# The first layer of the 128-row remainder tiles: four weight chunks in one accumulator bank, with one set of element-wise operations

## The chip, the cores and the metric

The kernel runs on one core of a Trainium2 chip. The metric is the device time of one execution in microseconds (us). The core has five engines, each with its own queue of instructions that it works off in order: TensorE (PE, matrix products, results in the PSUM accumulator memory; PEld is its loading of weights), VectorE (DVE), ScalarE (ACT), GpSimd (POOL) and SyncE (SP), which here issues the DMA transfers. PSUM is cut into banks of 512 fp32 columns on 128 partitions.

## What is computed

Two parts, one behind the other. First, causal attention with a decay on 8 batches of 8 heads, 576 rows and 64 columns per head. Second, on the 4608 x 512 result, a two-layer block with a hard-swish between the layers:

```python
scores = scale * np.matmul(q, k.transpose(0, 1, 3, 2))
decay = cum[:, :, :, None] - cum[:, :, None, :]          # cum: running sum of log f
attn = softmax(where(causal, -1e9, scores + decay))
x = matmul(attn, v)          # rearranged to 4608 rows x 512

h = x @ w_in                 # 512 -> 2048
relu6 = np.clip(h + 3.0, 0.0, 6.0)
g = h * relu6 / 6.0
out = g @ w_out              # 2048 -> 512
```

The kernel keeps fp32 accuracy with fp16 products: each operand is split into a high and a low fp16 part, and a product is three matmuls (high by high, high by low, low by high).

## The kernel before

The program goes through the heads one after another (`VH`). For each it emits the scores, the softmax, the transposition by DMA and the product with v. While it does this for batch b+1, the two-layer block of batch b is emitted in small units between the steps of the heads: `fill` keeps a credit, and lets the unit at the head of the list `units` advance by one `yield`, which costs the number yielded (`H_COST` is 1.05). The framework then settles the order of each engine's instructions with a simulated timeline, priorities and the free buffers, and sets the semaphores. The order on an engine is therefore near the program's, but two units, or a unit and a head, may be interleaved.

A batch has 576 rows, 512 + 64. `moe_tile` does the 512 rows: 16 units `h_unit` for the 16 chunks (`fc`) of 128 of the 2048 hidden columns, and then 4 units `out_unit` of 128 rows. The 64 rows left of two neighbouring batches are put together in the tile `xT[2]`, and `moe_rest(k)` does these 128 rows, with a column of scales for each batch. It is called four times: three times between the heads, after `moe_tile` of batch 1, 3 and 5, and once at the very end, where no attention is left. The profile names its tiles `ph_r`, `r_r` and `po_r`, those of `moe_tile` `ph`, `r` and `po`.

One `h_unit` consists of:

- 12 matmuls (lines 777 to 779; 4 chunks of 128 input columns, three products each) into one PSUM tile `ph` from `mm_tile`;
- for each segment of rows with a scale of its own, a Relu on ACT (line 784) from `ph` into the SBUF tile `r`. A full unit has one segment of 512, a unit of `moe_rest` two of 64;
- on DVE, the minimum with 6 and the product with `ph` (line 787). It is the last reader of the bank;
- on ACT, the copy to fp16, the high part of `gT` (line 789);
- on DVE, the low part of `gT`, as a difference (line 790). It is the last reader of `r`.

`out_unit` then multiplies `gT` by the second layer's weights, 48 matmuls of 512 columns (lines 800 to 802), in the order of the 16 chunks.

`mm_tile` hands out three banks: two in the pool `ps_m`, and at each third call the one of `ps_t`. The tile `r` has three buffers. A unit of `moe_rest` takes a whole bank and a whole buffer too, and uses 128 of its 512 columns. It yields 0.525, a full one 2 x 1.05.

Lines of the heads that the profile shows beside this: 611 and 614 (`pn`, scores on PE), 622 (mask and row maximum on DVE), 634 and 648 (exponential and fp16 copy on ACT), 651, 657 and 662 (low part, on DVE or POOL), 694 to 699 (`pav`, product with v, which waits for the transposing DMA `pT<-ring`), 399 and 400 (splitting v on ACT and DVE).

Of the kernel before, what the change touches and what calls it, by code (L numbers as in the profile page):

```python
# [11 lines left out]
F32 = mybir.dt.float32  # L12
F32R = mybir.dt.float32r
I32 = mybir.dt.int32
AF = mybir.ActivationFunctionType
ALU = mybir.AluOpType
# [4 lines left out]
def kernel(  # L21
# [10 lines left out]
    nc = tc.nc  # L32
# [7 lines left out]
    P = 128  # L40
# [4 lines left out]
    NCC = DM // P  # L45
    NFC = DFF // P
    TT = 512
# [3 lines left out]
    CG = 2.0 ** -22  # L51

    cpool = ctx.enter_context(tc.tile_pool(name="cpool", bufs=1))
    p2 = ctx.enter_context(tc.tile_pool(name="p2", bufs=2))
# [16 lines left out]
    bias_r = cpool.tile([P, 1], F32, name="bias_r")  # L71
# [11 lines left out]
    H_COST = 1.05  # L83
# [48 lines left out]
    w1 = [cpool.tile([P, NCC, DFF], F16, name=f"w1{i}") for i in range(2)]  # L132
    w2 = cpool.tile([P, NFC + 1, 2, DM], F16, name="w2")
    gT = cpool.tile([P, 2, NFC, TT], F16, name="gT")


    xT = [cpool.tile([P, NCC, TT // P, 2, P], F16, name=f"xT{i}") for i in range(3)]
# [13 lines left out]
    NG = 4  # L151
    SC = cpool.tile([P, 80], F32, name="SC")
    SV, IV, UO, UX, A1 = 0, 8, 16, 24, 32
# [47 lines left out]
    def scol(c):  # L201
        return SC[:, c:c + 1]
# [174 lines left out]
    def moe_scale_in(b, j):  # L377
        nc.vector.scalar_tensor_tensor(
            scol(A1 + NG * b + j), scol(IV + b), CG, scol(I1 + j), op0=ALU.mult, op1=ALU.mult
        )  # L380

    def moe_scale_out(b):
        nc.vector.scalar_tensor_tensor(
            scol(UO + b), scol(IV + b), 1.0 / (6.0 * CG), scol(I1R), op0=ALU.mult, op1=ALU.mult
        )
        nc.vector.tensor_tensor(scol(UO + b), scol(UO + b), scol(I2), op=ALU.mult)
        if b % 2 == 1:
            nc.vector.tensor_copy(SC[:64, UX + b:UX + b + 1], SC[:64, UO + b - 1:UO + b])
            nc.vector.tensor_copy(SC[64:, UX + b:UX + b + 1], SC[64:, UO + b:UO + b + 1])
# [196 lines left out]
    o = 0  # L586
# [176 lines left out]
    def mm_tile(name, three):  # L763

        turn[0] += 1
        if three and turn[0] % 3 == 0:
            return ps_t.tile([P, TT], F32, tag="tr", name=name)
        return ps_m.tile([P, TT], F32, tag="mm", name=name)

    def h_unit(x, fc, c0, c1, segs, three, name):  # L770

        nw = c1 - c0
        ph = mm_tile(f"ph_{name}_{fc}_{c0}", three)[:, :nw]
        fs_ = slice(fc * P, (fc + 1) * P)
        for cc in range(NCC):
            xh, xl = (x[:, cc, c0 // P:c1 // P, hl] for hl in range(2))
            nc.tensor.matmul(ph, w1[0][:, cc, fs_], xh, start=(cc == 0), stop=False)  # L777
            nc.tensor.matmul(ph, w1[0][:, cc, fs_], xl, start=False, stop=False)  # L778
            nc.tensor.matmul(ph, w1[1][:, cc, fs_], xh, start=False, stop=(cc == NCC - 1))  # L779
            if cc == 1 and nw == TT:  # L780
                yield H_COST
        r = p2.tile([P, TT], F32, tag="rt", name=f"r_{name}_{fc}_{c0}", bufs=3)[:, :nw]
        for a, e, b in segs:
            nc.scalar.activation(  # L784
                r[:, a:e], ph[:, a:e], AF.Relu, bias=bias_r, scale=scol(A1 + NG * b + fc * NG // NFC)
            )
        nc.vector.scalar_tensor_tensor(r, r, 6.0 * CG, ph, op0=ALU.min, op1=ALU.mult)  # L787
        g0 = c0 if x is not xT[2] else 0
        nc.scalar.copy(gT[:, 0, fc, g0:g0 + nw], r)  # L789
        nc.vector.tensor_tensor(  # L790
            gT[:, 1, fc, g0:g0 + nw], r, gT[:, 0, fc, g0:g0 + nw], op=ALU.subtract
        )
        yield H_COST if nw >= TT // 2 else H_COST / 2

    def out_unit(s, col, rows, three, name):

        po = mm_tile(f"po_{name}_{s}", three)
        ts_ = slice(s * P, (s + 1) * P)
        for fc in range(NFC):
            nc.tensor.matmul(po, gT[:, 0, fc, ts_], w2[:, fc, 0, :], start=(fc == 0), stop=False)  # L800
            nc.tensor.matmul(po, gT[:, 0, fc, ts_], w2[:, fc, 1, :], start=False, stop=False)  # L801
            nc.tensor.matmul(po, gT[:, 1, fc, ts_], w2[:, fc, 0, :], start=False, stop=(fc == NFC - 1))  # L802
            if fc % 2 and fc < NFC - 1:
                yield 2.0 - H_COST
        o = p2.tile([P, DM], F32, tag="o", name=f"o_{name}_{s}")
        nc.scalar.activation(o, po, AF.Copy, scale=scol(col))
        p = 0
        for r0, r1 in rows:
            nc.sync.dma_start(out[r0:r1, :], o[p:p + r1 - r0])
            p += r1 - r0  # L810
        yield 2.0 - H_COST

    def moe_tile(b, c0=0, c1=TT):

        for fc in range(NFC):
            j, new = divmod(fc, NFC // NG)
            if new == 0 and c0 == 0:
                while j not in w_in_done:
                    next(w_in_q, None)
                moe_scale_in(b, j)  # L820
            yield from h_unit(xT[b % 2], fc, c0, c1, [(0, c1 - c0, b)], b > 0 or c0 > 0, f"{b}")
        if b == 0:
            for _ in wq:
                pass
        if c0 == 0:
            moe_scale_out(b)
        for s in range(c0 // P, c1 // P):
            r = S * b + (64 if b else 0) + s * P
            yield from out_unit(s, UO + b, [(r, r + P)], b > 0 or s * P >= QA, f"{b}")

    def moe_rest(k):

        b = 2 * k
        for fc in range(NFC):
            yield from h_unit(
                xT[2], fc, k * P, (k + 1) * P, [(0, 64, b), (64, P, b + 1)], True, f"r{k}"
            )
        r = S - 64 if b == 0 else S * b
        yield from out_unit(0, UX + b + 1, [(r, r + 64), (S * (b + 1), S * (b + 1) + 64)], True, f"r{k}")

# [62 lines left out]
    def one(*a):  # L903
        yield from moe_tile(*a)

    def done(v):
        kind, n = VH[v]
        if kind == "A":
            if n == NPAIR - 1:
                units.append(one(0, 0, QA))  # L910
            return
        b, h = divmod(n, H)
        if h == H - 1:
            units.append(one(b, QA if b == 0 else 0, TT))
            if b % 2:
                units.append(moe_rest(b // 2))
# [4 lines left out]
    for i, (kind, n) in enumerate(VH):  # L921
        b, h = divmod(n, H)
        if kind == "A":
            b = h = 0
# [23 lines left out]
        ph = next(sg)  # L948
# [78 lines left out]
```

## Time and profile before

| | us |
|---|---|
| three runs | 1109.0 median, 1106.02 to 1109.42 |
| the profiled execution | 1104.82 |
| its span, first to last instruction | 1102.8 |
| PE busy in it | 1021.7 |
| DVE, ACT, POOL busy | 737.4, 619.0, 405.6 |

The mean granted PE clock of the profiled execution is 0.976. A busy time is the union of the times in which an engine had an instruction under way. Matmuls are pipelined: a row gives a matmul of 512 columns some 380 ns, though in an unbroken sequence the next one starts earlier, so rates are better read from starts. In the page's first part a row is an engine; in its second, the span is cut into 40 equal slices with a digit for the busy tenths of each.

### The profile page before, as it was taken

To read this page: it belongs to the slowest core of one execution; us is meant where nothing else is said; L and a number is where in the kernel's file an instruction comes from. 1 tells how busy PE (TensorE), PEld (TensorE's weight loads), DVE (VectorE), ACT (ScalarE), POOL (GpSimd) and SP (SyncE) were. 2 spreads that over 40 slices of the span, in tenths; PEclk is the share of its full clock that TensorE was granted. 3 is DMA by queue.
4 is the path that set the end of the run, shared out by engine and by line. 5 is a ranking of instruction groups with operands and counts; after the bars stand their busy time and mean duration, and the time that the engine had idled before them with its cause. 6 is when DMAs were issued, how large, how long until landed. Compare 5 with 4: busy or idle time off the path is not lost.

```text
span 1102.8 us, 21497 instructions
## 1 busy us (share of the span) xinstructions
PE 1021.7 (93%) x7650; PEld 612.0 (55%) x7650; DVE 737.4 (67%) x1983; ACT 619.0 (56%) x1333; POOL 405.6 (37%) x505
## 2 busy tenths in 40 slices
PE   2899977899999699999999799999999799999997
PEld 2677844755555655555555655555555655444445
DVE  7879899786967856867875767846895756305202
ACT  4778567655744765555744666545754756205205
POOL 7343566344444522444443632444443510000000
PEclk9889989999999999999999899999999999999999
DMA  8965557864866582567566781656657643100000
GB/s 255 295 183 181 141 125 147 187 135 95 180 129 134 124 182 50 116 138 166 114 132 131 151 167 39 122 124 171 119 118 139 110 81 57 26 29 10 1 29 20
DMA packets 259158, 133.80 MB, mean 121 GB/s; under 512 B 226948, under 2 KB 228540, under 8 KB 259052
## 3 DMA queue, kind: packets, MB, share of 16 engines
q1 hardware_dynamic: 259052, 132.44, 53.8%
q8 instruction: 60, 0.98, 0.4%
q14 instruction: 46, 0.38, 0.1%
HBM read 47.93 MB, written 9.73 MB: 52 GB/s over the span
## 4 chain that ended last, share of the span: by engine, by line
PE 73%; DVE 11%; DMA 5%; ACT 4%; issue 3%; POOL 2%; SPq 0%; ACTq 0%; DVEq 0%; POOLq 0%
PE ph L777 9%; PE ph L779 9%; PE ph L778 9%; PE po L800 9%; PE po L802 9%; PE po L801 9%; PE pn L611 3%; PE pn L614 3%; DMA pT<-ring 2%; DVE ring L651 2%; DVE pp L622 2%; PE po_r L800 1%; PE pav L705 1%; PE po_r L801 1%; PE po_r L802 1%
## 5 line engine op out<-in xcount | busy, mean ns | idle before, releaser
L634 ACT ACTIVATE pp<-pp,nb 128x192 f32<-128x192 f32 x280 | 138.7, 553 | 140.2 <-DVE nb L628 120.4
L777 PE MATMUL ph<-xT,w 128*128 128x512 f16 (+1 forms) x576 | 199.9, 358 | 1.5 <-DVE r L787 1.3
L801 PE MATMUL po<-w,gT 128*128 128x512 f16 x512 | 192.4, 382 | 8.9 <-DVE w L295 8.9
L779 PE MATMUL ph<-xT,w 128*128 128x512 f16 (+1 forms) x576 | 199.4, 357 | 0.0
L778 PE MATMUL ph<-xT,w 128*128 128x512 f16 (+1 forms) x576 | 199.1, 357 | 0.0
L800 PE MATMUL po<-w,gT 128*128 128x512 f16 x512 | 190.4, 383 | 3.7 <-DVE e_v L187 2.1
L802 PE MATMUL po<-w,gT 128*128 128x512 f16 x512 | 192.4, 382 | 0.0
L651 DVE TENSOR_TENSOR ring<-pp,ring 128x128 f16<-128x128 f32 (+2 forms) x216 | 130.2, 614 | 70.9 <-ACT ring L648 69.8
L787 DVE SCALAR_TENSOR_TENSOR r<-r,ph 128x512 f32<-128x512 f32 (+1 forms) x144 | 89.4, 621 | 96.2 <-ACT r L784 95.5
L622 DVE CUSTOM_DVE_ANT_0 pp<-pn,W 128x192 f32<-128x192 f32 x280 | 123.4, 482 | 30.8 <-PE pn L614 26.6
L461 POOL TENSOR_TENSOR T<-ST,T 64x576 fp32r<-64x576 f32 (+1 forms) x68 | 102.8, 1512 | 102.2 <-DMA T<-TK 87.5
L784 ACT ACTIVATE r<-ph,bias_r,SC 128x512 f32<-128x512 f32 (+1 forms) x144 | 104.0, 727 | 47.6 <-PE ph L779 45.8
L611 PE MATMUL pn<-TK,TQ 68*128 68x192 f32 x336 | 121.3, 376 | 8.1 <-issue 6.9
L790 DVE TENSOR_TENSOR gT<-r,gT 128x512 f16<-128x512 f32 (+1 forms) x144 | 105.9, 740 | 29.3 <-ACT gT L789 28.0
L778 PEld LDWEIGHTS <-w 128*128 128x128 f16 x832 | 82.6, 100 | 70.6 <-issue 25.4
L789 ACT CAST gT<-r 128x512 f16<-128x512 f32 (+1 forms) x144 | 81.4, 567 | 61.9 <-DVE r L787 61.5
L449 POOL TENSOR_SCALAR TK<-ST 64x576 fp32r<-64x576 f32 (+1 forms) x68 | 49.0, 721 | 181.6 <-PE pn L611 143.5
L648 ACT CAST ring<-pp 128x192 f16<-128x192 f32 x280 | 114.5, 452 | 1.5 <-DMA pT<-ring 1.5
L779 PEld LDWEIGHTS <-w 128*128 128x128 f16 x832 | 82.6, 100 | 56.9 <-issue 4.8
L614 PE MATMUL pn<-T,T 128*128 128x192 f32 x336 | 111.3, 358 | 0.2 <-POOL T L461 0.2
L777 PEld LDWEIGHTS <-w 128*128 128x128 f16 x832 | 81.2, 100 | 50.9 <-issue 8.5
L657 POOL TENSOR_TENSOR ring<-pp,ring 128x128 f16<-128x128 f32 x96 | 60.5, 630 | 129.1 <-ACT ring L648 89.8
(147 smaller groups left out, 2062.7 us busy)
## 6 DMA issues: line engine op xcount, KB each, us to landing
ST<-in_qk_dram SPq DMA_DIRECT2D x64, 288.0 KB
T<-TK SPq DMA_DIRECT2D x64, 144.0 KB
ring<-in_w_out_dram SPq DMA_DIRECT2D x16, 512.0 KB
out_dram<-o SPq DMA_DIRECT2D x32, 256.0 KB
T<-TQ SPq DMA_DIRECT2D x56, 144.0 KB
vst<-in_vS_dram SPq DMA_DIRECT2D x7, 1040.0 KB
ring<-in_w_in_dram SPq DMA_DIRECT2D x9, 512.0 KB
w<-in_w_in_dram SPq DMA_DIRECT2D x7, 512.0 KB
```

What stands on the lines that cost most here:

```text
L611: nc.tensor.matmul(dst, TQ[i][0:D + 4, qs], TK[i][0:D + 4, a:e], start=True, stop=False)
L614: nc.tensor.matmul(dst, T7[j][:, qs], T1[j][:, a:e], start=False, stop=True)
L622: nc.vector.tensor_tensor_reduce(pp[:r, w:w + kw], pn[:r, o:o + kw], W[:r, 4 * P + r - kw:4 * P + r], 1.0, -3.0e38, ALU.add, ALU.max, accu ...
L634: nc.scalar.activation(x_, x_, AF.Exp, bias=nb[:r, e0 + x:e0 + x + 1], scale=0.125)
L648: nc.scalar.copy(hl[:r, h0[c]:h0[c] + kw], pp[:r, at[c]:at[c] + kw])
L651: eng.tensor_tensor(hl[:r, a:a + c * P], pp[:r, at[c] + 64:at[c] + kw], hl[:r, h0[c] + 64:h0[c] + kw], op=ALU.subtract,)
L777: nc.tensor.matmul(ph, w1[0][:, cc, fs_], xh, start=(cc == 0), stop=False)
L778: nc.tensor.matmul(ph, w1[0][:, cc, fs_], xl, start=False, stop=False)
L779: nc.tensor.matmul(ph, w1[1][:, cc, fs_], xh, start=False, stop=(cc == NCC - 1))
L800: nc.tensor.matmul(po, gT[:, 0, fc, ts_], w2[:, fc, 0, :], start=(fc == 0), stop=False)
L801: nc.tensor.matmul(po, gT[:, 0, fc, ts_], w2[:, fc, 1, :], start=False, stop=False)
L802: nc.tensor.matmul(po, gT[:, 1, fc, ts_], w2[:, fc, 0, :], start=False, stop=(fc == NFC - 1))
```

## The change

`h_unit` loses the list of segments and does full tiles alone. A new `rest_unit` takes the place of the 16 small units of `moe_rest`: 4 units, each of which puts four chunks (`fc` = 4j to 4j+3) side by side in the 512 columns of one bank, one after the other, each with its own 12 matmuls of 128 columns. The element-wise operations then run once over all 512 columns. As the scale depends on the batch, and each chunk's 128 columns hold 64 of one batch and 64 of the other, each of the two Relus reads and writes four runs of 64 columns. The scale depends on the chunk only through its group of four, so one column of scales fits the unit. The copy and the difference write 4 x 128 columns of `gT`, with 512 between the starts of two runs.

```diff
-    def h_unit(x, fc, c0, c1, segs, three, name):
+    def h_unit(x, fc, c0, c1, b, three, name):
...
-        for a, e, b in segs:
+        nc.scalar.activation(
+            r, ph, AF.Relu, bias=bias_r, scale=scol(A1 + NG * b + fc * NG // NFC)
+        )
+        nc.vector.scalar_tensor_tensor(r, r, 6.0 * CG, ph, op0=ALU.min, op1=ALU.mult)
+        nc.scalar.copy(gT[:, 0, fc, c0:c1], r)
+        nc.vector.tensor_tensor(gT[:, 1, fc, c0:c1], r, gT[:, 0, fc, c0:c1], op=ALU.subtract)
+        yield H_COST
+
+    def rest_unit(k, j):
+
+        n = NFC // NG
+        ph = mm_tile(f"ph_r{k}_{j}", True)
+        for i in range(n):
+            fs_ = slice((n * j + i) * P, (n * j + i + 1) * P)
+            dst = ph[:, i * P:(i + 1) * P]
+            for cc in range(NCC):
+                xh, xl = (xT[2][:, cc, k, hl] for hl in range(2))
+                nc.tensor.matmul(dst, w1[0][:, cc, fs_], xh, start=(cc == 0), stop=False)
+                nc.tensor.matmul(dst, w1[0][:, cc, fs_], xl, start=False, stop=False)
+                nc.tensor.matmul(dst, w1[1][:, cc, fs_], xh, start=False, stop=(cc == NCC - 1))
+            if i == n // 2 - 1:
+                yield H_COST
+        r = p2.tile([P, TT], F32, tag="rt", name=f"r_r{k}_{j}", bufs=3)
+        r3, p3 = (t.rearrange("p (f t) -> p f t", t=P) for t in (r, ph))
+        for i in range(2):
+            o = slice(64 * i, 64 * i + 64)
             nc.scalar.activation(
-                r[:, a:e], ph[:, a:e], AF.Relu, bias=bias_r, scale=scol(A1 + NG * b + fc * NG // NFC)
+                r3[:, :, o], p3[:, :, o], AF.Relu, bias=bias_r,
+                scale=scol(A1 + NG * (2 * k + i) + j),
             )
         nc.vector.scalar_tensor_tensor(r, r, 6.0 * CG, ph, op0=ALU.min, op1=ALU.mult)
...
-        yield H_COST if nw >= TT // 2 else H_COST / 2
+        hi, lo = (gT[:, hl, n * j:n * (j + 1), 0:P] for hl in range(2))
+        nc.scalar.copy(hi, r3)
+        nc.vector.tensor_tensor(lo, r3, hi, op=ALU.subtract)
+        yield H_COST
...
-        for fc in range(NFC):
-            yield from h_unit(
-                xT[2], fc, k * P, (k + 1) * P, [(0, 64, b), (64, P, b + 1)], True, f"r{k}"
-            )
+        for j in range(NG):
+            yield from rest_unit(k, j)
```

More of the change, by code (lines that the diff above doesn't have):

```diff
@@ L782, in h_unit @@
         r = p2.tile([P, TT], F32, tag="rt", name=f"r_{name}_{fc}_{c0}", bufs=3)[:, :nw]
-        for a, e, b in segs:
+        nc.scalar.activation(
[22 more added lines that the diff above has]
+            o = slice(64 * i, 64 * i + 64)
             nc.scalar.activation(
-                r[:, a:e], ph[:, a:e], AF.Relu, bias=bias_r, scale=scol(A1 + NG * b + fc * NG // NFC)
+                r3[:, :, o], p3[:, :, o], AF.Relu, bias=bias_r,
+                scale=scol(A1 + NG * (2 * k + i) + j),
             )
         nc.vector.scalar_tensor_tensor(r, r, 6.0 * CG, ph, op0=ALU.min, op1=ALU.mult)
[L788 to L791, printed above, removed]
-        )
-        yield H_COST if nw >= TT // 2 else H_COST / 2
+        hi, lo = (gT[:, hl, n * j:n * (j + 1), 0:P] for hl in range(2))
+        nc.scalar.copy(hi, r3)
+        nc.vector.tensor_tensor(lo, r3, hi, op=ALU.subtract)
+        yield H_COST
     def out_unit(s, col, rows, three, name):
@@ L820, in moe_tile @@
                 moe_scale_in(b, j)
-            yield from h_unit(xT[b % 2], fc, c0, c1, [(0, c1 - c0, b)], b > 0 or c0 > 0, f"{b}")
+            yield from h_unit(xT[b % 2], fc, c0, c1, b, b > 0 or c0 > 0, f"{b}")
         if b == 0:
@@ L833, in moe_rest @@
         b = 2 * k
-        for fc in range(NFC):
-            yield from h_unit(
-                xT[2], fc, k * P, (k + 1) * P, [(0, 64, b), (64, P, b + 1)], True, f"r{k}"
-            )
+        for j in range(NG):
+            yield from rest_unit(k, j)
         r = S - 64 if b == 0 else S * b
```

## The prediction

> **What bounds the kernel now.** I read the busy rows and the row of granted clock on the page first, then the busy time by stretches, cut where a digit of the PE row falls. Columns of the stretches: stretch, its length, then busy time (count) of PE, PEld, DVE, ACT and POOL, granted clock, DMA share, GB/s.
>
> ```profile
> PE 1021.7 (93%) x7650; PEld 612.0 (55%) x7650; DVE 737.4 (67%) x1983; ACT 619.0 (56%) x1333; POOL 405.6 (37%) x505
> PE   2899977899999699999999799999999799999997
> 355.00:410.00 55.00, 45.86 (x490) 33.53 (x489) 37.68 (x117) 36.23 (x99) 24.69 (x34) 0.94 0.77 157
> 410.00:600.00 190.00, 190.00 (x1388) 103.41 (x1387) 137.91 (x355) 108.75 (x216) 73.91 (x97) 1.00 0.57 119
> 600.00:660.00 60.00, 52.03 (x530) 35.97 (x529) 40.10 (x124) 38.78 (x103) 30.62 (x40) 0.94 0.81 167
> 660.00:850.00 190.00, 188.59 (x1372) 102.73 (x1371) 136.99 (x354) 106.54 (x213) 76.91 (x100) 1.00 0.55 117
> 850.00:910.00 60.00, 51.82 (x511) 36.22 (x510) 38.21 (x118) 38.46 (x102) 23.05 (x29) 0.94 0.55 100
> ```
>
> Between 410 and 850 us PE is the bound: never idle for 190 us, then for 1.4 of 190. It loses time in three places only, 355-410, 600-660 and 850-910: 9.14 + 7.97 + 8.18 = 25.3 us idle. These are where the three middle calls of `moe_rest` run. Who makes PE wait is in the table of waits (total, times, longest), over the whole span:
>
> ```profile
> PE ph_r L777 <- DVE r_r L787: 18.3, 11, 5.8
> PE pn L611 <- issue: 6.9, 2, 4.7
> PE pav L694 <- DMA pT<-ring: 7.7, 9, 2.0
> ```
>
> The first is the step that changes: a short unit's first matmul waits until line 787 has read the bank of an earlier unit. The time-ordered rows of the longest such wait, DVE's first, then ACT's, then PE's, say why:
>
> ```profile
> 365.96 0.27 DVE L787 SCALAR_TENSOR_TENSOR r_r<-r_r,ph_r 128x128 f32<-128x128 f32 x1
> ...
> 367.88 1.69 DVE L400 SCALAR_TENSOR_TENSOR v<-vst,SC,v 128x320 f16<-128x320 f32 x1
> 369.49 2.12 DVE L790 TENSOR_TENSOR gT<-r_r,gT 128x128 f16<-128x128 f32 x3
> 371.53 2.19 DVE L651 TENSOR_TENSOR ring<-pp,ring 128x256 f16<-128x256 f32 x2
> 373.64 0.47 DVE L787 SCALAR_TENSOR_TENSOR r_r<-r_r,ph_r 128x128 f32<-128x128 f32 x2
> ```
>
> ```profile
> 371.07 1.88 ACT L784 ACTIVATE r_r<-ph_r,bias_r,SC 128x64 f32<-128x64 f32 x6 [1.90 <-DVE gT L790]
> ```
>
> ```profile
> 373.97 0.26 PE L777 MATMUL ph_r<-xT,w 128*128 128x128 f16 x1 [5.83 <-DVE r_r L787]
> ```
>
> DVE comes back to a short unit only 7.4 us after 366.23 (365.96 + 0.27), because the work of a head stands between in its queue. Three banks and three `r` buffers are all the slack there is. Two rows of one unit, its first and its twelfth matmul, price that slack:
>
> ```profile
> 1086.86 0.22 PE L777 MATMUL ph_r<-xT,w 128*128 128x128 f16 x1 [0.33 <-DVE r_r L787]
> ...
> 1087.47 0.22 PE L779 MATMUL ph_r<-xT,w 128*128 128x128 f16 x1
> ```
>
> Eleven steps in 0.61 us are 0.0555 us a matmul, 0.67 us a unit: three banks hold 2.0 us of PE work against a 7.4 us absence of DVE.
>
> **The change part by part.** PE's work stays: 192 matmuls of 128 columns per rest, then the 48 of `po_r`. The turn counter moves by 4 in place of 16, both 1 modulo 3, so later units keep their banks; yields add up to 8.4 either way (16 x 0.525, 8 x 1.05). No DMA is added, moved or removed.
>
> *Operations.* Groups by shape (busy, mean ns):
>
> ```profile
> L784 ACT ACTIVATE r_r<-ph_r,bias_r,SC 128x64 f32<-128x64 f32 x128 | 42.4, 405 | 11.9 <-DVE gT L790 5.7 <-PE ph_r L779 4.1 <-PE pn L614 1.8
> L784 ACT ACTIVATE r<-ph,bias_r,SC 128x256 f32<-128x256 f32 x32 | 17.7, 560 | 9.9 <-PE ph L779 8.3 <-PE ptm L502 1.3
> L789 ACT CAST gT<-r_r 128x128 f16<-128x128 f32 x64 | 17.5, 305 | 8.6 <-DVE r_r L787 8.6
> L789 ACT CAST gT<-r 128x512 f16<-128x512 f32 x112 | 68.9, 615 | 52.9 <-DVE r L787 52.5
> L787 DVE SCALAR_TENSOR_TENSOR r_r<-r_r,ph_r 128x128 f32<-128x128 f32 x64 | 17.4, 278 | 48.4 <-ACT r_r L784 47.0 <-PE ph_r L779 1.2
> L787 DVE SCALAR_TENSOR_TENSOR r<-r,ph 128x512 f32<-128x512 f32 x112 | 76.3, 681 | 92.7 <-ACT r L784 92.2
> L790 DVE TENSOR_TENSOR gT<-r_r,gT 128x128 f16<-128x128 f32 x64 | 24.3, 403 | 5.5 <-ACT gT L789 5.4
> L790 DVE TENSOR_TENSOR gT<-r,gT 128x512 f16<-128x512 f32 x112 | 88.8, 796 | 26.7 <-ACT gT L789 25.3
> ```
>
> Per rest, a quarter of the busy times, ACT did (42.4 + 17.5) / 4 = 15.0 us and now does 8 x 0.560 + 4 x 0.615 = 6.9; DVE did (17.4 + 24.3) / 4 = 10.4 and now does 4 x (0.681 + 0.796) = 5.9. Neither engine is the bound, so the 8.1 and 4.5 us saved count only through PE's waits. No row shows a Relu over four runs of 64 columns: the 256-column row, 0.560, is the low bound, four starts of the 64-column row, 1.62, the high one. I take 0.560, the row with the same number of elements. At 1.62 the Relus cost 13.0 us per rest, no less than before, and only the buffers and DVE gain. The strided write of the copy lies likewise between 0.615 and 4 x 0.305 = 1.22; I take 0.615.
>
> *Waits.* A bank now holds 48 x 0.0555 = 2.66 us of PE work, three of them 8.0 us: just over DVE's 7.4 us, and a head's own matmuls come on top. Units of 512 columns live with the same three banks, under the same heads, in this stretch, with DVE at 82%:
>
> ```profile
> 505.00:560.00 55.00, 55.00 (x414) 30.24 (x413) 45.18 (x109) 38.05 (x74) 25.47 (x34) 1.00 0.65 144
> ```
>
> PE is never idle there. So I cost the middle waits of `ph_r` at nothing from now on; that cover is gone if DVE stays away for over 8 us.
>
> *Clock.* Five stretches around these waits ran at half clock (same columns; the last row sums the busy times, PE first):
>
> ```profile
> 373.32:376.74 3.42, 2.77 (x25) 2.77 (x25) 3.42 (x16) 1.48 (x6) 0.82 (x2) 0.50 1.07 198
> ...
> sum 20.48, PE 16.82 PEld 16.80 DVE 19.85 ACT 13.29 POOL 6.39; mean PE 3.36 PEld 3.36 DVE 3.97 ACT 2.66 POOL 1.28
> ```
>
> PE was busy for 16.82 of these 20.48 us at half speed, so 8.4 us would not have been needed at full clock. The Trainium skill, "TensorE: Matmul & The Clock Gate", section "Part 1: The HAM clock gate", says that the clock drops to half after an idle window of about 3.4 us, and prices the loss as the throttled time times one half. By it the clock term would be 10.2, an estimate from that page, in place of 8.4; the 0.50 and the 3.42 us in the row agree with it.
>
> *The last rest* (1075-1088) has no head beside it. The stretch of its first layer, with the columns as above, and the same for the tile `ph_r` alone (PE, DVE, ACT):
>
> ```profile
> 1074.95:1087.53 12.58, 11.01 (x182) 10.29 (x181) 6.67 (x26) 12.33 (x43) 0.00 (x0) 1.00 0.06 23
> ```
>
> ```profile
> 1074.95:1087.53 12.58, 11.01 (x180) 4.04 (x14) 9.28 (x30) 1.00 0.06 23
> ```
>
> The first and the last matmul of the `po_r` behind them:
>
> ```profile
> 1087.53 0.38 PE L800 MATMUL po_r<-w,gT 128*128 128x512 f16 x1
> ...
> 1097.67 0.38 PE L802 MATMUL po_r<-w,gT 128*128 128x512 f16 x1
> ```
>
> ACT, busy 12.33 of 12.58 us, sets the pace. 180 x 0.0555 = 10.0 us is what PE needs; with ACT at 6.9 us for the whole rest, PE sets the pace: 2.6 us saved. `po_r` takes 0.216 us a matmul (10.14 us over 47 steps) and needs the last unit only at its 37th of 48, so that unit's longer chain (2 x 0.560 + 0.681 + 0.615 + 0.796 = 3.2 us) is hidden behind 36 x 0.216 = 7.8 us of `po_r`; unhidden it would cost 3.2.
>
> *The sum.* Ceiling: 25.3 + 8.4 + 2.6 = 36.3 us. Not all of it goes. Two other waits of PE lie in the three stretches: one of `pn` and four of `pav` for the transposing DMA. The table of waits for 355 to 910 us has them:
>
> ```profile
> PE pn L611 <- issue: 4.7, 1, 4.7
> PE pav L694 <- DMA pT<-ring: 3.1, 4, 1.4
> ```
>
> I leave both in, 4.7 + 3.1 = 7.8 us, and nothing for the clock behind them: 36.3 - 7.8 = 28.5, taken as **28 us**. The profiled execution took 1104.8 us (span 1102.8), the median of the runs is 1109.0; taken off the median, 1081.
>
> **The rivals.**
> *DVE takes the bank's place.* Stalled PE time also let DVE catch up. If the heads come sooner, DVE's queue may hold PE at `pn`, as in the 4.7 us row. For it: DVE is full for 19.85 of 20.48 us in the half-clock stretches. Against it: 4.5 us less DVE work per rest, and the 505-560 row. If each rest keeps one such wait of 4.7 us and the clock loss of 8.4 stays, 36.3 - 14.1 - 8.4 = 13.8 us are gained: 1095.
> *Nothing gained but the tail.* The strided Relus cost 1.62 each, or the order of the program changes so that banks are no help: 2.6 us, 1106.
> *Slower: the wait moves to gT.* `po_r` stands in PE's queue ahead of the next head. A unit visits DVE twice after its Relus, and each visit may wait out a 7.4 us absence: the last unit's gT then lands 3.2 + 14.8 = 18 us after its matmuls, and PE, covered for 7.8, waits 10.2. With a third absence ahead of the Relus (the `r` buffers) it is 17.6, x 3 = 52.8 us, and 8.4 of clock are lost again: 1109.0 - 36.3 + 61.2 = 1134. It decides from (36.3 - 8.4) / 3 = 9.3 us of wait per rest on. Against it: `gT` releases PE nowhere in the table of waits, though full units take the same road.
>
> **How the numbers follow.** Forecast 0.65, 1072 to 1091 (all of the ceiling to half of it gone); beyond the ceiling 0.05; DVE takes the place 0.14, 1091 to 1104; nothing but the tail 0.07; slower 0.09. The range 1070 to 1103 takes in the forecast and nearly all of the DVE case, 0.8. A measurement here tells 0.3%, 3.3 us, from no change. Faster 0.65 + 0.05 + 0.14 = 0.84, same 0.07, slower 0.09.
>
> **What would show it.** Right: 16 units of 48 `ph_r` matmuls, no wait of PE on DVE `r_r` over 1 us, granted clock 1.00 in the three stretches, Relus of 256 at 0.56, and 10 us for the last rest's `ph_r`. The prediction is wrong if PE's idle time near the rests stays over 15 us under another name (`pn`, `pT`, `gT`), or if these Relus take over 1 us.

## The result and the profile after

| | before | after |
|---|---|---|
| runs, median | 1107.5 us (4 runs, 1103.0 to 1109.4) | 1073.5 us (4 runs, 1071.0 to 1075.1) |
| the profiled execution | 1104.82 | 1071.03 |
| its span | 1102.8 | 1069.2 |

The ratio is 0.970, with a 95% interval of 0.968 to 0.972: 34 us less. The forecast was 28 us less.

The first parts of the page of the changed kernel, the busy row and PE's busy tenths, and then three stretches around the middle calls of `moe_rest`, in the columns that the prediction used:

```profile
PE 1011.8 (95%) x7650; PEld 603.8 (56%) x7650; DVE 730.3 (68%) x1887; ACT 587.0 (55%) x1189; POOL 402.7 (38%) x505
PE   2799978999999999999999999999999999999996
```

```profile
355.00:410.00 55.00, 55.00 (x551) 35.98 (x550) 41.38 (x100) 35.24 (x72) 24.29 (x31) 1.00 0.69 142
590.00:650.00 60.00, 59.78 (x596) 39.10 (x593) 45.74 (x110) 36.58 (x74) 26.05 (x33) 1.00 0.68 145
830.00:885.00 55.00, 55.00 (x552) 35.96 (x550) 41.20 (x100) 34.91 (x71) 18.14 (x24) 1.00 0.52 95
```

The 6 and the 7s in the middle of PE's row have become 9s. PE is idle for 0.2 us in the three stretches together, and the granted clock is 1.00 in all of them. The table of waits of the changed kernel for 340 to 960 us, which takes in all three middle calls, has three rows:

```profile
PE po L824 <- DVE e_v L187: 0.8, 1, 0.8
PE po L824 <- ACT o L830: 0.8, 1, 0.8
PE ph_r L800 <- DVE r_r L813: 0.2, 1, 0.2
```

The waits of `ph_r` are gone, and so are those of `pn` (4.7) and `pav` (3.1), which the prediction left in. The new operations, from the groups by shape of the changed kernel:

```profile
L809 ACT ACTIVATE r_r<-ph_r,bias_r,SC 128x256 f32<-128x256 f32 x32 | 16.0, 560 | 20.0 <-PE ph_r L802 20.0
L816 DVE TENSOR_TENSOR gT<-r_r,gT 128x512 f16<-128x512 f32 x16 | 11.7, 741 | 3.3 <-ACT gT L815 3.2
L813 DVE SCALAR_TENSOR_TENSOR r_r<-r_r,ph_r 128x512 f32<-128x512 f32 x16 | 10.7, 681 | 62.7 <-ACT r_r L809 62.7
L815 ACT CAST gT<-r_r 128x512 f16<-128x512 f32 x16 | 9.7, 620 | 9.6 <-DVE r_r L813 9.6
```

A Relu over four runs of 64 takes 560 ns, exactly as one over 256 columns in a row.

**Where the time came from.** A stage here runs from the first `ph_r` matmul of one call of `moe_rest` to that of the next. The first stage of each kernel as a stretch, before's first and the changed kernel's behind it:

```profile
360.00:608.70 248.70, 239.56 (x1899) 138.58 (x1897) 177.53 (x475) 146.08 (x317) 103.00 (x136) 0.99 0.61 128
```

```profile
356.30:592.70 236.40, 236.40 (x1900) 135.27 (x1898) 174.62 (x451) 137.87 (x281) 104.73 (x136) 1.00 0.65 135
```

The work of PE is the same (1899 and 1900 records). Of the 12.3 us gained, 9.1 are idle time of PE (248.70 - 239.56) that is no longer there, and 3.2 are busy time that shrank (239.56 to 236.40), since none of it runs at half clock now. All stages of the two profiled executions:

| us | start of the first call | first stage | second stage | third call to the end | span |
|---|---|---|---|---|---|
| before | 360.0 | 248.7 | 249.6 | 244.5 | 1102.8 |
| after | 356.3 | 236.4 | 238.1 | 238.4 | 1069.2 |
| difference | -3.7 | -12.3 | -11.5 | -6.1 | -33.6 |

The start of the first call lies between 354 and 361 us in all the kernels below, none of which changes anything ahead of it, so its -3.7 is read as scatter. The last column but one has both the third middle call and the last one. If the third gives about as much as the first two, the last call must have **cost** some 6 us, where the prediction had it save 2.6.

That can be seen at the end of the changed kernel, in the rows in order of time, PE's first, then ACT's, then DVE's:

```profile
1046.66 0.27 PE L800 MATMUL ph_r<-xT,w 128*128 128x128 f16 x1 [3.29 <-DVE r_r L813]
```

```profile
1043.36 2.85 ACT L809 ACTIVATE r_r<-ph_r,bias_r,SC 128x256 f32<-128x256 f32 x6 [6.58 <-PE ph_r L802]
1046.07 1.79 ACT L815 CAST gT<-r_r 128x512 f16<-128x512 f32 x3
1058.93 1.02 ACT L809 ACTIVATE r_r<-ph_r,bias_r,SC 128x256 f32<-128x256 f32 x2 [11.08 <-PE ph_r L802]
```

```profile
1045.32 1.88 DVE L813 SCALAR_TENSOR_TENSOR r_r<-r_r,ph_r 128x512 f32<-128x512 f32 x3 [49.39 <-ACT r_r L809]
```

Three units have their six Relus in one group: all three were finished by PE at the same moment, though they could have been finished one after the other. ACT had been idle for 6.58 us before, and PE then waits 3.29 us for the first bank. The stretch behind that wait, in the columns of before:

```profile
1046.66:1050.10 3.44, 3.44 (x28) 3.02 (x28) 2.35 (x4) 1.20 (x3) 0.00 (x0) 0.50 0.02 5
```

It ran at half clock. The fourth unit's matmuls are then spread among those of `po_r` and end only at 1058.9, so that its chain over ACT and DVE is not covered: `po_r` waits 2.5 us for `gT`.

### The profile page after: what moved, and what is told of

It is laid out like the page before. It is cut to its first block, busy times and chain, and to the rows that moved or that the text cites. A ratio compares the mean times of both kernels' runs of the same rounds, so it can differ in the third digit from the quotient of the medians.

```text
span 1069.2 us, 21155 instructions
## 1 busy us (share of the span) xinstructions
PE 1011.8 (95%) x7650; PEld 603.8 (56%) x7650; DVE 730.3 (68%) x1887; ACT 587.0 (55%) x1189; POOL 402.7 (38%) x505
## 4 chain that ended last, share of the span: by engine, by line
PE 77%; DVE 9%; DMA 5%; ACT 5%; issue 3%; POOL 1%; SPq 0%; ACTq 0%; DVEq 0%; POOLq 0%
PE po L824 9%; PE po L826 9%; PE po L825 9%; PE ph L777 9%; PE ph L779 9%; PE ph L778 9%; PE pn L614 3%; PE pn L611 3%; DMA pT<-ring 2%; DVE pp L622 1%; PE pav L698 1%; DVE ring L651 1%; PE pav L699 1%; PE pav L697 1%; PE po_r L826 1%
## 5 line engine op out<-in xcount | busy, mean ns | idle before, releaser
L651 DVE TENSOR_TENSOR ring<-pp,ring 128x128 f16<-128x128 f32 (+2 forms) x216 | 137.2, 646 | 86.8 <-ACT ring L648 86.2
L461 POOL TENSOR_TENSOR T<-ST,T 64x576 fp32r<-64x576 f32 (+1 forms) x68 | 99.9, 1469 | 105.8 <-DMA T<-TK 97.0
L611 PE MATMUL pn<-TK,TQ 68*128 68x192 f32 x336 | 125.3, 386 | 1.6 <-issue 1.0
L788 DVE TENSOR_TENSOR gT<-r,gT 128x512 f16<-128x512 f32 (+1 forms) x144 | 109.6, 767 | 21.3 <-ACT gT L787 19.5
L614 PE MATMUL pn<-T,T 128*128 128x192 f32 x336 | 115.3, 368 | 1.9 <-DMA pT<-ring 1.6
L458 POOL TENSOR_TENSOR T<-ST,TQ 64x576 fp32r<-64x576 f32 (+2 forms) x68 | 97.2, 1430 | 17.1 <-PE pn L614 11.5
L826 PEld LDWEIGHTS <-gT 128*128 128x128 f16 x576 | 56.4, 98 | 75.2 <-issue 13.6
L825 PEld LDWEIGHTS <-gT 128*128 128x128 f16 x576 | 56.6, 99 | 66.5 <-issue 10.1
```

Of the source, the lines that this page charges most:

```text
L611: nc.tensor.matmul(dst, TQ[i][0:D + 4, qs], TK[i][0:D + 4, a:e], start=True, stop=False)
L614: nc.tensor.matmul(dst, T7[j][:, qs], T1[j][:, a:e], start=False, stop=True)
L651: eng.tensor_tensor(hl[:r, a:a + c * P], pp[:r, at[c] + 64:at[c] + kw], hl[:r, h0[c] + 64:h0[c] + kw], op=ALU.subtract,)
```

## The experiments

The questions were two. At the end: is it the order of the units or the longer chain of a wide unit that costs time? In the middle: which part of the change gives the gain, the bank for four chunks (the prediction's 8.0 us of work against DVE's absence of 7.4), the buffer `r` for four chunks, or the wider operations of ACT and of DVE? Kernels of one group below were timed beside the same runs of before.

### The last call alone, and all but the last call

In `e1_old_tail` the last call keeps the 16 short units of before; in `e2_new_tail_only` it is the one call that has the new ones.

```diff
-        for j in range(NG):
+        for j in range(NG if k < 3 else 0):
             yield from rest_unit(k, j)
+        for fc in range(NFC if k == 3 else 0):
+            yield from small_unit(k, fc)
```

> The changed kernel, but with the 16 short units of before in the last call of moe_rest, the one at the end; the three middle calls have four chunks in a bank. Theory A: at the end the change costs time, because the order planned there lets three wide units advance together, so that all three banks fill and none is free until PE has waited 3.3 us (and run 3.4 us at half clock) and po_r has waited 2.5 us for gT. From the copy of the third last output tile on ACT to the end the profiles show 36.8 us before and 42.3 us after, so the old end would take 5.5 us off: 1068, ratio to before 0.964. Theory B, as the prediction had it: the change saves 2.6 us at the end, so the old end costs 2.6 us: 1076, ratio 0.972.

> The counterpart: the kernel before, with four chunks in a bank only in the last call of moe_rest. Theory A: 5.5 us slower than before, 1113, ratio 1.005, with PE waits of about 3 us on DVE r_r and 2.5 us on ACT gT in the last 30 us. Theory B: 2.6 us faster, 1105, ratio 0.998.

Measured: `e1_old_tail` 1068.9 us, ratio 0.967 (0.965 to 0.970); `e2_new_tail_only` 1113.1, ratio 1.006 (1.003 to 1.008), with before at 1105.8. The times are medians; the ratios are of means, and the differences that follow are taken from the ratios. So the three middle calls give 36.4 us (33.7 to 39.1), and the last one costs 6.2 (3.8 to 8.6). Both kernels came out as their theory A had it. Together that is 30.2, about the 34 of the whole change. PE's waits behind 1040 us in the second kernel have the same two rows as the changed kernel's tail:

```profile
PE ph_r L800 <- DVE r_r L813: 3.3, 1, 3.3
PE po_r L845 <- ACT gT L815: 2.5, 1, 2.5
```

### The units in the order of the program

The operations stay those of the change. In `e3_tail_in_order` the first matmul of each unit of the last call, and the first of its `po_r`, are kept in the program's order, so that the framework can't let several units advance in turn. `e8_all_in_order` does the same in all four calls (`True` and `name[0] == "r"` for the two conditions).

```diff
-                nc.tensor.matmul(dst, w1[0][:, cc, fs_], xh, start=(cc == 0), stop=False)
+                first = nc.tensor.matmul(dst, w1[0][:, cc, fs_], xh, start=(cc == 0), stop=False)
+                if k == 3 and i == cc == 0:
+                    tc.keep_in_program_order(first)
...
-            nc.tensor.matmul(po, gT[:, 0, fc, ts_], w2[:, fc, 0, :], start=(fc == 0), stop=False)
+            first = nc.tensor.matmul(po, gT[:, 0, fc, ts_], w2[:, fc, 0, :], start=(fc == 0), stop=False)
+            if name == "r3" and fc == 0:
+                tc.keep_in_program_order(first)
```

> The changed kernel, with the first matmul of each unit of the last call of moe_rest, and that of its second layer, kept behind all that was traced before it on PE, so that the four units finish one after another. Theory A: the two waits of PE at the end go (no wait of PE on r_r or gT there over 0.5 us, clock 1.00 until PE is done), and the last stage falls from 42.3 to about 34.2 us, which is that of before (36.8) less the 2.6 us that its short units cost: 1065.4, ratio 0.962. Theory B: order is not the cause, the long chain of a wide unit is (2 x 0.56 + 0.68 + 0.62 + 0.8 us): the waits stay, 1073, ratio 0.970.

> As the run before, but with all four calls of moe_rest kept in order, so that in the middle, too, a unit's 48 matmuls begin only behind what was traced before them. Theory A: nothing waits in the middle either way (the changed kernel shows 0.3 us at most there), so that it comes out as the run before, 1065, within 2 us. Rival: the free interleaving of units with the heads is what hides the heads' waits in the middle, and pinning it costs 2 us or more in each of the three places: 1072 or more, with waits of PE on pav or pn in the three stretches.

Measured: 1064.2 us, ratio 0.963 (0.961 to 0.965), and 1066.3, ratio 0.964 (0.961 to 0.967). Both came out as their theory A had it, both beat the changed kernel (0.970, 0.968 to 0.972), and `e3_tail_in_order` has the lowest median of all: 41.6 us under before. ACT's rows at its end:

```profile
1042.65 1.02 ACT L811 ACTIVATE r_r<-ph_r,bias_r,SC 128x256 f32<-128x256 f32 x2 [1.95 <-PE ph_r L804]
1044.42 0.62 ACT L817 CAST gT<-r_r 128x512 f16<-128x512 f32 x1 [0.75 <-DVE r_r L815]
1045.33 1.02 ACT L811 ACTIVATE r_r<-ph_r,bias_r,SC 128x256 f32<-128x256 f32 x2 [0.29 <-PE ph_r L804]
...
1050.69 1.02 ACT L811 ACTIVATE r_r<-ph_r,bias_r,SC 128x256 f32<-128x256 f32 x2 [0.29 <-PE ph_r L804]
```

A unit's Relus come every 2.68 us, which is the time of its 48 matmuls (48 x 0.0555 = 2.66). PE waits for nothing of `ph_r` or `gT` there. The chain of a unit is as long as in the change, and hidden; the order alone was the cost. In the middle, order is worth nothing: the first two stages of `e8_all_in_order` are 236.4 and 237.8 us, those of the change 236.4 and 238.1.

### The bank for four chunks with the small operations, and the buffer `r` alone

`e4_wide_bank_small_ops` keeps the four chunks in one bank and in one `r`, but runs 8 Relus of 64 columns and four products, copies and differences of 128.

```diff
+        for i in range(n):
+            fc, c = n * j + i, slice(i * P, (i + 1) * P)
+            for h in range(2):
+                o = slice(i * P + 64 * h, i * P + 64 * h + 64)
+                nc.scalar.activation(
+                    r[:, o], ph[:, o], AF.Relu, bias=bias_r, scale=scol(A1 + NG * (2 * k + h) + j)
+                )
+            nc.vector.scalar_tensor_tensor(
+                r[:, c], r[:, c], 6.0 * CG, ph[:, c], op0=ALU.min, op1=ALU.mult
+            )
+            nc.scalar.copy(gT[:, 0, fc, 0:P], r[:, c])
+            nc.vector.tensor_tensor(gT[:, 1, fc, 0:P], r[:, c], gT[:, 0, fc, 0:P], op=ALU.subtract)
```

`e5_r_for_four` gives each chunk its own bank, as before, with the same small operations, and only lets four chunks share one buffer `r`. `e7_small_banks_wide_gT` is the same with the copy and the difference done once over the four chunks. `e6_two_banks` is the changed kernel with two banks in place of three.

```diff
+        r = p2.tile([P, TT], F32, tag="rt", name=f"r_r{k}_{j}", bufs=3)
+        r3 = r.rearrange("p (f t) -> p f t", t=P)
         for i in range(n):
+            ph = mm_tile(f"ph_r{k}_{j}_{i}", True)[:, :P]
```

```diff
-        ph = mm_tile(f"ph_r{k}_{j}", True)
+        ph = mm_tile(f"ph_r{k}_{j}", False)
```

> Four chunks in a bank as in the changed kernel, but all element-wise operations per chunk as before (8 Relus of 64 columns, 4 each of the others of 128 columns, all behind the 48 matmuls of the bank). It tells the bank apart from the number of operations. Measure: the time from the first ph_r matmul of the first call of moe_rest to that of the second, 248.7 us before and 236.4 after, and PE's idle time and half-clock stretches between. Theory bank: what counted was PE work held ready (three banks of 2.66 us against DVE's absences of 7.4 us); 12 us per call go, up to 2 less for the longer chains: 236 to 239. Theory operations: what counted was the load of 48 more instructions on ACT and DVE per call; 245 or more.

> The kernel before with one alteration in the short units: four chunks share one buffer of r (each in 128 of its 512 columns), so that three buffers hold 12 chunks in place of 3. Banks of 128 used columns and all operations as before. In the longest wait of before the Relus stood behind the buffers of r. Theory bank: three banks of 0.67 us still empty in 2 us, so the stage from first call to second stays at 245 to 249 us. Theory buffers of r: they were what held the banks; the stage falls to 240 or less.

> As the run before it (four chunks share a buffer of r, a bank for each chunk), and the copy to gT and the difference done once for four chunks: 12 fewer instructions on ACT and 12 fewer on DVE per call, the banks as before. Theory bank: 244 us or more for the stage from first call to second. Theory operations: it gets half or more of the 12.3 us, 242 or less.

> The changed kernel, with the units of moe_rest using two banks in place of three (the pool of two, never the third). Theory bank: two banks hold 5.3 us of PE work, less than DVE's absences of 7.4 us, so waits of PE on r_r come back, 2 to 4 us in each of the three middle stretches: 1080 to 1086 in all, stage 239 to 241. Theory operations: the same stage as the changed kernel, 236.4.

Since the last call differs too, the first two stages are the cleaner measure. Before's were taken twice: 248.7 and 249.6 in its own profile, 250.2 and 250.6 in `e2_new_tail_only`, whose middle is that of before. Differences under 1.5 us are not read. The last column takes all three middle calls together, from the first `ph_r` matmul to the last `pav` matmul; for before it is 584.2 and, in `e2_new_tail_only`, 587.7, and for the four kernels with the change's middle (after, `e1_old_tail`, `e3_tail_in_order`, `e8_all_in_order`) 548.5 to 549.7.

| | us, ratio to before (1106.6) | first stage | second stage | three calls |
|---|---|---|---|---|
| before | | 248.7 | 249.6 | 584.2 |
| `e5_r_for_four` | 1095.9, 0.991 (0.988 to 0.994) | 246.4 | 246.5 | 574.6 |
| `e7_small_banks_wide_gT` | 1089.0, 0.984 (0.980 to 0.987) | 243.6 | 245.6 | 569.2 |
| `e4_wide_bank_small_ops` | 1098.0, 0.992 (0.989 to 0.995) | 242.1 | 245.3 | 566.4 |
| after | | 236.4 | 238.1 | 549.0 |
| `e6_two_banks` | 1068.6, 0.965 (0.962 to 0.969) | 236.3 | 237.6 | 548.1 |

The buffer alone gives 2.3 and 3.1 us of the stages, the bank with it 6.6 and 4.3; over the three calls that is 9.6 and 17.8 us of the change's 35.2, so the bank with the buffer is worth half of it. The shared buffer with the wide copy and difference, without the wide bank (`e7_small_banks_wide_gT`), comes to 15.0. Theory bank holds for `e5_r_for_four` alone (245 to 249 for the first stage); `e4_wide_bank_small_ops` and `e7_small_banks_wide_gT` miss both of their theories, and `e6_two_banks` has the stage of theory operations. In the waits of 340 to 960 us of `e4_wide_bank_small_ops` no `ph_r` stands any more, yet PE still waits:

```profile
PE po_r L825 <- DVE r_r L813: 5.8, 1, 5.8
PE pav L694 <- DMA pT<-ring: 4.4, 4, 1.6
```

So with the bank and the small operations PE waits further down: at `po_r` in the second call, at `pav` in the other two. And three banks are not needed: `e6_two_banks` loses nothing in the middle, with 2 x 2.66 = 5.3 us of work in two banks. DVE's rows in its first middle call:

```profile
370.33 0.68 DVE L813 SCALAR_TENSOR_TENSOR r_r<-r_r,ph_r 128x512 f32<-128x512 f32 x1
...
379.51 0.69 DVE L813 SCALAR_TENSOR_TENSOR r_r<-r_r,ph_r 128x512 f32<-128x512 f32 x1 [0.16 <-ACT r_r L809]
```

The stretch between them, and the same for the tile `ph_r` alone (PE, DVE, ACT):

```profile
371.01:379.51 8.50, 8.50 (x151) 8.07 (x149) 5.99 (x14) 5.27 (x13) 5.76 (x8) 1.00 0.70 162
```

```profile
371.01:379.51 8.50, 5.52 (x96) 0.00 (x1) 1.01 (x2) 1.00 0.70 162
```

Between two of its readings of a bank lie 8.5 us, and PE is busy without a gap: 96 of its 151 matmuls are `ph_r`, just the two units that two banks hold, and the other 55 are the heads' and a full unit's. Banks and absence alone, 5.3 against 8.5, would make it 3.2 us idle. (The later of the two readings is not late through DVE here: the two units are worked on in turn among the other matmuls, PE finishes them at 377.2, and ACT starts their Relus at 378.46, behind a head's operations.) The last call has the units in pairs in this kernel, and 231.5 us from the third call to the end, 6.9 under the change.

### Which engine's operations

`e9_wide_act_small_dve` has the change's two Relus and one copy, and the product and the difference in four parts of 128. `e10_small_act_wide_dve` is the reverse. `e11_one_bank` is the changed kernel with the bank of `ps_t` alone for `ph_r`. `e12_small_units_in_order` has before's short units in all four calls, kept in order as above.

```diff
-        nc.vector.scalar_tensor_tensor(r, r, 6.0 * CG, ph, op0=ALU.min, op1=ALU.mult)
+        for i in range(n):
+            c = slice(i * P, (i + 1) * P)
+            nc.vector.scalar_tensor_tensor(
+                r[:, c], r[:, c], 6.0 * CG, ph[:, c], op0=ALU.min, op1=ALU.mult
+            )
...
-        nc.vector.tensor_tensor(lo, r3, hi, op=ALU.subtract)
+        for i in range(n):
+            nc.vector.tensor_tensor(lo[:, i], r3[:, i], hi[:, i], op=ALU.subtract)
```

```diff
-        for i in range(2):
+        for i in range(2 * n):
             o = slice(64 * i, 64 * i + 64)
             nc.scalar.activation(
-                r3[:, :, o], p3[:, :, o], AF.Relu, bias=bias_r,
-                scale=scol(A1 + NG * (2 * k + i) + j),
+                r[:, o], ph[:, o], AF.Relu, bias=bias_r,
+                scale=scol(A1 + NG * (2 * k + i % 2) + j),
             )
...
-        nc.scalar.copy(hi, r3)
+        for i in range(n):
+            nc.scalar.copy(hi[:, i], r3[:, i])
```

```diff
-        ph = mm_tile(f"ph_r{k}_{j}", True)
+        turn[0] += 1
+        ph = ps_t.tile([P, TT], F32, tag="tr", name=f"ph_r{k}_{j}")
```

```diff
-        for j in range(NG):
-            yield from rest_unit(k, j)
+        for fc in range(NFC):
+            yield from small_unit(k, fc)
```

> Four chunks in a bank, ACT's operations as in the changed kernel (2 Relus, 1 copy per bank), DVE's per chunk (4 products and 4 differences of 128 columns per bank). With all operations small the stage from the first call of moe_rest to the second was 242.1 us, with all wide 236.4. Theory DVE: the number of DVE's visits, each behind a head's operations in its queue, makes the difference: 240 to 242. Theory ACT: the 36 more operations on ACT make it: 236 to 238.

> The counterpart: four chunks in a bank, ACT's operations per chunk (8 Relus of 64 columns, 4 copies of 128), DVE's wide. Theory DVE: 236 to 238 for the stage from first call to second. Theory ACT: 240 to 242. If both this run and the one before it lie near 239, the load counts on either engine.

> The changed kernel, with one bank for all units of moe_rest. Three banks and two banks gave the same stage, 236.4 and 236.3 us. Theory slack: below some point PE must wait for the product of DVE before the next unit, some 2 us of Relus and product and up to a 7.4 us absence for each of three units in a call: stage 242 to 255, total 1085 or more. Rival: the planned order fills PE with other ready work (heads, second layer of the tile before), and one bank does as well: 236 to 239.

> The kernel before (16 short units, a bank for each), with the first matmul of each short unit and of its second layer kept behind what was traced before it on PE. It tells the order apart from the operations. Theory operations: the stage from first call to second stays at 246 us or more, since all short operations remain. Rival, order: the units crowding ahead of the heads made the waits, and in order the stage falls to 241 or less.

| | us, ratio to before (1106.8) | first stage | second stage | three calls |
|---|---|---|---|---|
| `e9_wide_act_small_dve` | 1074.7, 0.971 (0.967 to 0.975) | 237.4 | 237.7 | 549.4 |
| `e10_small_act_wide_dve` | 1085.6, 0.982 (0.977 to 0.986) | 238.4 | 241.5 | 554.2 |
| `e11_one_bank` | 1082.0, 0.978 (0.974 to 0.982) | 238.2 | 243.9 | 557.7 |
| `e12_small_units_in_order` | 1099.1, 0.994 (0.992 to 0.995) | 247.5 | 252.0 | 581.4 |

With the wide bank, ACT's part alone takes the stages from 242.1 and 245.3 to 237.4 and 237.7: the change's own, within the scatter, as theory ACT had it. DVE's part alone leaves 238.4 and 241.5, the first of which lies between its two theories. Over the three calls, where the bank with small operations has 566.4 and the change 549.0, ACT's part brings 17.0 us and DVE's 12.2. The two overlap, and ACT's is the larger. Rows of one unit, first of ACT in `e4_wide_bank_small_ops`, then of DVE in `e9_wide_act_small_dve`, show what an operation costs:

```profile
366.77 1.28 ACT L810 ACTIVATE r_r<-ph_r,bias_r,SC 128x64 f32<-128x64 f32 x4
367.94 0.30 ACT L816 CAST gT<-r_r 128x128 f16<-128x128 f32 x1
```

```profile
369.44 0.88 DVE L815 SCALAR_TENSOR_TENSOR r_r<-r_r,ph_r 128x128 f32<-128x128 f32 x4
372.19 0.88 DVE L821 TENSOR_TENSOR gT<-r_r,gT 128x128 f16<-128x128 f32 x4
```

On ACT, a unit's 8 small Relus and 4 small copies are 2 x 1.28 + 4 x 0.30 = 3.8 us, the wide ones 2 x 0.560 + 0.620 = 1.7: 2.0 us less. On DVE, four small products in a row take 0.88 us and the wide one 0.68, four differences 0.88 and the wide one 0.74: 0.3 us less. This DVE unit is a quick one: another group of four differences of the same kernel, at 374.61, took 2.57 us. Over all 16 units the busy times of the groups are 64.7 us on ACT and 46.2 on DVE with small operations (`e4_wide_bank_small_ops`), 26.1 on ACT and 22.7 on DVE where they are wide (`e9_wide_act_small_dve`, `e10_small_act_wide_dve`), so that the wide ones save 2.4 us a unit on ACT and 1.5 on DVE. That the size of the saving makes ACT count more fits these numbers; a kernel that varies ACT's time by itself was not run.

One bank costs 1.8 and 5.8 us against the change, and 8.7 over the three calls, no more, though it makes every unit wait for DVE to have read the one before: the first stage is that of the rival, the second that of theory slack. And the order by itself, with the short units, gives next to nothing in the middle, as theory operations had it: 247.5 and 252.0 against before's 248.7 and 249.6, and 2.8 us over the three calls, less than the 3.5 by which before's two profiles differ. At the end it gives 1.2 us: from the start of the third last copy of an output tile on ACT to the end it is 35.6 us, before 36.8. The profiled executions differ by 3.8 us, the medians by 7.8; what is left of these was not taken apart.

## Why the prediction was right or wrong

It was right in sign and in time (1081 with a range of 1070 to 1103; 1073.5 measured). Two of its steps were off and in part made up for each other, so that the total comes closer than its terms: that is luck.

- **The bound.** PE's idle time in the three stretches, named as the prize, was the prize: 9.1 us of it went in the first stage, and nothing took its place. Right.
- **The operations.** The Relu at 0.560, the low of two bounds, measured 0.560; the copy 0.620 for 0.615; the product 0.681 as said; the difference 0.741 for 0.796. In the first stage ACT's busy time fell by 8.2 us (8.1 predicted), DVE's by 2.9 (4.5 predicted); DVE's two groups themselves fell by 4.8 a call, from 41.7 to 22.4 over the four, and other work on DVE took longer (line 651 over the whole span 137.2 us in place of 130.2). Right, but the step that followed, that neither counts for itself, was wrong: with the wide bank and the old operations half of the gain is missing, and ACT's alone bring nearly all of it back.
- **The waits.** "Costed at nothing" was right as a figure: 0.2 us of `ph_r` in the middle. Its reason, that three banks hold 8.0 us and so just outlast 7.4, was wrong: two banks with 5.3 us cause no wait either, as PE has other matmuls to do between the units, and with three of them and the old operations PE waits 5.8 us at `po_r` all the same. Nor were the 7.4 us an absence that a head's work alone made. Line 790 in the prediction's own rows is the short units': DVE was at them again at 369.49, and ACT's next Relus stood behind line 790, that is behind a buffer `r`. And some 3.5 of the 7.4 us are the excess of three stretched operations of DVE: 1.69 us of line 400, 1.48 of the first of line 790's three, 1.75 of line 651's second, against medians of 0.55, 0.28 and 0.54 of the same operations where no two-input operation of POOL runs beside them (last section).
- **The 7.8 us left in** (`pn` and `pav`): this is the term that was mis-sized. Both waits are gone in the change, 0 measured. The middle calls gave 36.4 us (33.7 to 39.1, from `e1_old_tail`) where the terms for them came to 25.9, and to 33.7 with nothing left in. In `e5_r_for_four`, where PE still waits on `ph_r`, a wait of `pn` of 4.0 us and waits of `pav` of 3.5 in all are there too. In `e4_wide_bank_small_ops`, which has no wait of `ph_r`, `pn`'s is gone, but `pav` still waits 4.4; with either engine's operations wide as well (`e9_wide_act_small_dve`, `e10_small_act_wide_dve`) neither waits. So `pav`'s wait hangs on the small operations at least in part, not on `ph_r` alone; by what path was not tested.
- **The clock.** Half clock in the middle is gone altogether, as taken. PE's busy time in the first stage fell by 3.2 us. Its two half-clock stretches held 2.77 and 2.94 us of busy PE, half of which is 2.9. The rule of the Trainium skill, "TensorE: Matmul & The Clock Gate", "Part 1: The HAM clock gate", gives 3.4 from their 6.84 us, an estimate. The measurement lies between and doesn't decide.
- **The last call, "2.6 us saved"**: this step failed. It cost 6.2 us (3.8 to 8.6). The prediction counted what ACT and PE need, and took it that the units come one after the other. They came three at a time, which left ACT idle for 6.58 us and then PE for 3.29, and half clock behind it. With the units in order the figure comes back: from `e1_old_tail` to `e3_tail_in_order`, old tail to new, the time from the third call to the end falls from 232.8 to 230.4, which is 2.4 us. But half of that is the order's: from the third last copy of an output tile on ACT to the end it is 36.8 us with the short units, 35.6 with them in order (`e12_small_units_in_order`), and 34.3 with the wide units in order, so that the wide operations themselves save 1.3.
- **The rivals.** DVE in the bank's place, nothing but the tail, and a wait moved to `gT` did not come about in the middle. The last has a trace at the end, where `po_r` does wait 2.5 us for `gT`, by another mechanism than the one given: the late fourth unit, with DVE free.
- **What would show it.** 16 units, granted clock of 1.00, Relus of 0.56 and no long wait in the middle: all there. "No wait of PE on DVE `r_r` over 1 us" failed at the end (3.29), and with it "10 us for the last rest's `ph_r`": it took 1029.3 to 1058.7. In `e3_tail_in_order` it took 1039.8 to 1050.4, 10.6 us.

So the sum was 28 = 25.9 + 2.6, rounded, and the runs have 36.4 for the first and -6.2 for the second: 30.2, and 34.0 for the change as a whole, whose own runs were not taken beside these. A middle 10.5 us better and an end 8.8 us worse than the terms nearly cancel.

## What to carry to other kernels

Fewer and wider element-wise operations on an engine that is only half busy can be worth more than the buffers that seem to be missing (here one bank with wide operations took 557.7 us over the three calls, three banks with small ones 566.4): ask what one unit's operations take on each engine, not only how many units fit between. Wider units of equal priority need a look at their order: where the framework may advance several at once, they fill all buffers and finish together, and the engine behind them has nothing to do until then. A work count for the end of a kernel, where nothing else covers, holds only for the order that was assumed.

## What the runs showed of the hardware

An ACT operation over four strided runs of 64 columns cost the same 560 ns as one over 256 columns in a row; the further runs inside an operation cost nothing that the profile shows, at least for four.

Behind a single wait of 3.29 us lies a half-clock stretch of 3.44 us, although PE had been busy with gaps of under 1 us since 340 us. PE works through all of that stretch, with a matmul of 128 columns every 0.107 us in place of 0.0555, so the wait costs some half of 3.44 us on top of its own 3.29.

The same operation of DVE has very different durations. Two rows in a row of `e6_two_banks`, one operation each:

```profile
372.80 1.89 DVE L816 TENSOR_TENSOR gT<-r_r,gT 128x512 f16<-128x512 f32 x1
...
374.68 0.68 DVE L816 TENSOR_TENSOR gT<-r_r,gT 128x512 f16<-128x512 f32 x1
```

In that time POOL runs one of its long sums:

```profile
372.62 1.52 POOL L458 TENSOR_TENSOR T<-ST,TQ 64x576 fp32r<-64x576 f32 x1
```

The long one lies beside it, the short one behind its end (374.14). The same can be seen in the longest wait of before, where POOL runs these beside the stretched rows of DVE that the prediction shows:

```profile
367.50 1.72 POOL L458 TENSOR_TENSOR T<-ST,TQ 64x576 fp32r<-64x576 f32 x1
369.29 1.53 POOL L461 TENSOR_TENSOR T<-ST,T 64x576 fp32r<-64x576 f32 x1
371.84 1.47 POOL L461 TENSOR_TENSOR T<-ST,T 64x576 fp32r<-64x576 f32 x1
```

In the whole trace of the changed kernel no such stretch is without it: of the 128 differences of 512 columns (lines 788 and 816), both inputs of which are in SBUF, the 95 that overlap no TENSOR_TENSOR of POOL took 643 to 694 ns, the 33 that do 673 to 1895. The 128 products of 512 columns (lines 786 and 813), which read one input from PSUM, took 641 to 690 ns either way. So the stretch goes with POOL's two-input operations and with two inputs in SBUF; a kernel with POOL's work moved was not run.
